# An odd-frequency transform of the sequence's own length in a long convolution, with the order of its pieces rewritten

## The chip, the cores and the metric

The kernel runs on one core of one Trainium2 chip. Its engines are TensorE (PE in the profile; PEld is its weight load), VectorE (DVE), ScalarE (ACT), GpSimd (POOL) and SyncE (SP). The metric is the device time of one execution in microseconds (us), lower is better. All times here are in us unless marked ns, and a place in the profile is the time since the span's first instruction.

## The reference

```python
def _attn_ref(x, h):                      # x (8, 5696, 128), h (5696, 128)
    L = 2 * S
    Xf = np.fft.rfft(x, n=L, axis=1)
    Hf = np.fft.rfft(h, n=L, axis=0)
    y = np.fft.irfft(Xf * Hf[None], n=L, axis=1)[:, :S, :]
    return y

def _moe_ref(x, w_theta, w_tok_r, w_tok_i, w_ch):
    theta = x @ w_theta
    zr, zi = x * np.cos(theta), x * np.sin(theta)
    y = einsum('ts,bsd->btd', w_tok_r, zr) + einsum('ts,bsd->btd', w_tok_i, zi)
    u = x + y
    return u + np.maximum(u @ w_ch, 0.0)
```

A causal convolution along the 5696 positions of each of 8 x 128 sequences comes first, and its result goes through the second block. The change is in the convolution alone.

## The kernel before

**The convolution** is a transform written as matmuls. A sequence is laid out as NB = 89 rows of N2 = 64, zero-padded to NF = 11392 = 178 x 64, and K1 = 90 of the 178 outer frequencies are kept (the sequence is real). A group is two batches and half of the channels (HD = 64), so there are 8 groups, `groups[0]` to `groups[7]`. Each group goes through four stages, each cut into pieces. Every piece takes one PSUM buffer from `psum()`, a pool `fp` of four buffers of two banks each, fills it with matmuls, and has it emptied by one engine:

- **A**, the input pieces (`stage_a`, matmul L251): 16 pieces of 4 matmuls, over the 89 rows. ACT empties them (L258); `on_dve` names pieces that DVE empties instead (L256). Before the change these are pieces 5 and 11 of group 1 and none of a later group.
- **B**, the spectrum pieces (`stage_b` and `f2`, L269): 12 pieces over K1, eight outer frequencies each (the last has two). ACT copies a piece to `xs` (L399), and DVE multiplies it twice with the spectrum of h into `u_t` and `v_t` (L401). Behind the last piece's matmuls, still into that piece's buffer, stand WARM = 12 matmuls whose result is not used (L275).
- **C**, first half of the inverse (`stage_c`, L421 and L422): 16 pieces of 16 matmuls, which read `u_t` and `v_t` over all outer frequencies, so the first C piece waits for the last B piece's DVE products. A piece leaves PSUM multiplied with a table of signs and halves, `sgn`: on DVE as one product (L429), or on ACT as two scaled copies (L426, L427). ACT has pieces 8, 10, 12 and 14, in the last group all eight even ones.
- **D**, second half of the inverse (`stage_d`, L444): 7 pieces, each of which reads all C pieces of its group; ACT empties them into `yt` (L447), and behind the seventh SP stores `yt`.

**The order** is what the loop over groups near L755 writes, and PE, ACT and DVE execute these pieces in that order. `woven` merges lists by giving each entry a place in a share of the stretch. For group g one stretch holds the 16 C pieces of g and the 16 A pieces of g + 1 in the first 55% of it (with `load_x(g + 2)` behind the A pieces), and the next stretch holds the 12 B pieces of g + 1 and the 7 D pieces of g. The first stretch is called C/A here, the second B/D. Before the change the rounds of C/A hold one or two A pieces and a C piece, and B/D runs B0 D0 B1 B2 D1 B3 B4 D2 B5 B6 D3 B7 D4 B8 B9 D5 B10 B11 D6. Three A pieces stand ahead of the first C piece.

`load_x` (L138) brings the next input in 16 transfers on POOL's queue, into a single buffer, so it starts when the A pieces have read the one before.

**After the convolution** the last group's C and D pieces are woven with phase steps (`phase_step`: sines and cosines on ACT, L537 to L539), and the mixing follows: from about 540 us on, PE's matmuls of L1262 and their helpers fill the time.

Of the kernel before, what the change touches and what calls it, by code (L numbers as in the profile page):

```python
# [10 lines left out]
F32 = mybir.dt.float32  # L11
# [12 lines left out]
def kernel(  # L24
# [52 lines left out]

    NF = 2 * S
    N2 = 64
    N1 = NF // N2  # L80
    NB = S // N2
    K1 = N1 // 2 + 1
    KH = K1 // 2
    CK = 8
    HD = D // 2
    EN = N2 // 2 + 1
    WARM = 12
    XP = HD + 4
    assert N1 * N2 == NF and NB * N2 == S and NB % 2 == 1 and K1 <= P
    CHK = [(c0, min(CK, K1 - c0)) for c0 in range(0, K1, CK)]  # L90
    NCK = len(CHK)
    CN = 10
    CHN = [(c0, min(CN, N2 - c0)) for c0 in range(0, N2, CN)]
    UVW = 2 * HD * K1
    hf_hbm = nc.dram_tensor("hf_hbm", (P, HD * K1), F16, kind="Internal").ap()
# [24 lines left out]
    v_t = fc.tile([P, UVW + P], F16)  # L120
    uv = [t[:, :UVW].rearrange("p (e d k) -> p e d k", e=2, k=K1) for t in (u_t, v_t)]
    h16 = s1.tile([P, 2, N2, HD], F16)
# [24 lines left out]
    for p0 in (0, 64):  # L147
# [3 lines left out]
                   allow_small_or_imprecise_dtypes=True)  # L151
    nc.vector.memset(lane[0:64, 2:3], 0.0)
    nc.vector.memset(lane[64:P, 2:3], float(KH))

# [18 lines left out]

    w_t2 = keep.tile([P, K1, 3 * N2], F16, tag="keep", name="w_t2")
    assert WB + BT + 3 * P * 2 <= K1 * 3 * N2
    f1_t = fc.tile([P, 2 * K1], F16)
# [27 lines left out]
    def w_rest(b):  # L204
        s0 = WS * b
        here = w_t2[:, s0:s0 + WS]
        two = here[:, :, :2 * N2].rearrange("p k (f a n) -> p k f a n", f=2, a=2)
        nc.vector.tensor_scalar(two[:, :, :, 1], two[:, :, :, 0], odd, None, op0=mult)
        nc.vector.tensor_scalar(here[:, :, 2 * N2:], here[:, :, :N2], -1.0, None, op0=mult)
        for p0 in (0, 64):  # L210
            nc.vector.tensor_copy(w_t2[p0:p0 + 64, KH + s0:KH + s0 + WS],
                                  w_t2[64 - p0:P - p0, s0:s0 + WS])

    nc.scalar.activation(f1_t[:, :1], zero_b, AF.Sin, bias=zero_b)
    for b in range(len(w_of)):
        index(w_of[b][1], [[1, WS], [N1, 32]], WS * b)
        if b == 0:
            index(f_k, [[1, K1]], 0)
    nc.vector.tensor_scalar(lane[:, 3:4], lane[:, 0:1], 1.0 / NF, None, op0=mult)
    nc.vector.tensor_scalar(o_t, lane[:, 1:2], 0.5, None, op0=mult)  # L220
# [4 lines left out]
    w_turns(0)  # L225
    nc.vector.tensor_scalar(f_t, f_k, lane[:NB, 1:2], 1.0 / N1, op0=mult, op1=mult)
    up(f_t, f_k)
# [32 lines left out]

    def f2(a_st, c, warm=True):

        c0, ck = CHK[c]
        ps = psum()
        for j in range(ck):
            for ri in range(2):
                for e in range(2):
                    rows = slice(64 * e, 64 * e + 64)
                    nc.tensor.matmul(ps[:, e, j * HD:(j + 1) * HD],  # L269
                                     w_t2[rows, slot(e, c0 + j), N2 * (1 - ri):N2 * (3 - ri)],  # L270
                                     a_st["a"][rows, ri * K1 + c0 + j, :],
                                     start=(ri == 0), stop=(ri == 1))
        if c == NCK - 1 and warm:
            for n in range(WARM):
                nc.tensor.matmul(ps[:, n % 2, ck * HD:ck * HD + 384], w_t2[:, 2, :P],  # L275
                                 w_t2[:, 0:2, :].rearrange("p k n -> p (k n)"), start=True, stop=True)
        return ps[:, :, :ck * HD].rearrange("p e (k d) -> p e d k", k=ck)
# [21 lines left out]

    nc.gpsimd.memset(u_t[:, UVW:], 0.0)  # L300
    nc.gpsimd.memset(v_t[:, UVW:], 0.0)
    HS = [(0, 4)] + [(c, 1) for c in range(4, NCK)]
# [21 lines left out]
    def h_chunk(c):  # L324
        c0, ck = CHK[c]
        ps = f2(a_h, c, False)
        nc.scalar.activation(h_part(c)[:, 0], ps[:, 0], AF.Copy, scale=16.0 / NF)
        nc.vector.tensor_scalar(h_later[:, HD * c0:HD * (c0 + ck)].rearrange("p (d k) -> p d k", k=ck),
                                ps[:, 1], 16.0 / NF, None, op0=mult)

# [11 lines left out]
    e_t = fc.tile([P, EN, 2, NB], F16)  # L342
    sgn = fc.tile([P, N2], F32)

    def r_table(n_, r_):
# [9 lines left out]
        sine(k, t, 1)  # L355
        nc.scalar.activation(r_[:, :N2 + EN], k[:, :N2 + EN], AF.Copy, scale=0.125)
        nc.scalar.activation(r_[:, N2 + EN:], k[:, N2 + EN:], AF.Copy, scale=-0.125)

# [10 lines left out]
    def e_index(n, n0, cn):  # L369
        t, k = e_pair(n, cn)  # L370
        index(k, [[1, cn], [N2, NB]], n0)
        nc.gpsimd.tensor_scalar(t, k, lane[:K1, 1:2], 1.0 / NF, op0=mult, op1=mult)
        up(t, k, nc.gpsimd)
# [8 lines left out]

    def s_table():
        half, end = lane[:, 5:6], lane[:, 6:7]
        nc.vector.tensor_scalar(half, lane[:, 1:2], 0.0, -0.5, op0=ALU.is_equal, op1=mult)
        nc.vector.tensor_scalar(end, lane[:, 1:2], float(K1 - 1), -0.5, op0=ALU.is_equal, op1=mult)
        nc.vector.scalar_tensor_tensor(half, half, 1.0, end, op0=add, op1=add)
        nc.vector.memset(sgn, 1.0)
        nc.vector.tensor_scalar(sgn[:, :EN], sgn[:, :EN], half, None, op0=mult)
        nc.vector.tensor_scalar(sgn[:, EN:], sgn[:, EN:], odd, half, op0=mult, op1=mult)  # L390

    def stage_b(a_st, warm, refill):

        def chunk(c):
            c0, ck = CHK[c]
            hv = h_part(c)
            ps = f2(a_st, c, warm)
            xs = fs.tile([P, 2, HD, CK], F16, tag="xs", name="xs")
# [11 lines left out]

    def stage_c(st, last):
        sg = sgn[:K1].unsqueeze(2).unsqueeze(1).to_broadcast([K1, 2, N2, 8])

        def chunk(q):
            if q == 0:
                st["g"] = fg.tile([P, 2 * N2, P], F16, tag="g", name="g_")
            ps = psum()
            for i in range(8):
                o = ps[:, i // 4, (i % 4) * P:(i % 4 + 1) * P]
                at = (q + i) * K1  # L420
                nc.tensor.matmul(o, u_t[:, at:at + P], r_u, start=True, stop=False)  # L421
                nc.tensor.matmul(o, v_t[:, at:at + P], r_v, start=False, stop=True)  # L422
            g_out = st["g"][:K1, :, q:q + 8].rearrange("p (r n) q -> p r n q", r=2)
            g_in = ps[:K1].rearrange("p a (q r n) -> p r n (a q)", q=4, r=2)
            if q % 16 == 0 and (last or q >= 64):
                nc.scalar.mul(g_out[:, :, :EN], g_in[:, :, :EN], sgn[:K1, 0:1])  # L426
                nc.scalar.mul(g_out[:, :, EN:], g_in[:, :, EN:], sgn[:K1, EN:EN + 1])  # L427
            else:
                nc.vector.tensor_tensor(g_out, g_in, sg, op=mult)  # L429
        return [lambda q=q: chunk(q) for q in range(0, 2 * HD, 8)]  # L430

    def stage_d(st, bp, dh, then=None):
        def chunk(n0, cn):
# [5 lines left out]
            for j in range(cn):  # L439
                n = n0 + j  # L440
                o = ps[:, j // nq, (j % nq) * NB:(j % nq + 1) * NB]
                for ri in range(2):
                    e_ = e_t[:K1, n, ri, :] if n < EN else e_t[:K1, N2 - n, ri, ::-1]
                    nc.tensor.matmul(o, g_[:K1, ri * N2 + n, :], e_, start=(ri == 0), stop=(ri == 1))  # L444
# [15 lines left out]
    def front(g, on_dve=()):  # L460
# [4 lines left out]
        steps, a_st = stage_a(lambda q: x16[:NB, :, q], on_dve)  # L465
        return steps, stage_b(a_st, g > 0, dh == 0 and groups[g + 1][1] == 1)

# [13 lines left out]
    for n, f in enumerate(a0):  # L481
        f()
        if n == 9:
# [4 lines left out]
    in_order.enter_context(tc.manual_schedule(engines={mybir.EngineType.DVE, mybir.EngineType.Activation}))  # L488
    woven(b0, ([s_table, lambda: r_table(0, r_u), lambda: r_table(1, r_v)], 0.0, 0.6),
          [])  # L490
    e_left = [lambda f=f, n=n: f(*E_STEPS[n]) for f, n in (
# [117 lines left out]
    def open_ring():  # L609

        ring["all"] = keep.tile([P, K1 * 3 * N2], BF16, tag="keep", name="ring")
        pump()
# [142 lines left out]
    for g, (bp, dh) in enumerate(groups):  # L755
        st = {}
        last = g + 1 == len(groups)
        if last:
            late_order.enter_context(tc.manual_schedule(engines={mybir.EngineType.Pool}))
        a_, b_ = front(g + 1, () if g else (5, 11))  # L760
        if last:
            for _ in range(3):
                steps0.pop(0)()
        now = [with_load(steps0.pop(0), n < 6) for n in range(9)] if last else []
        c_ = stage_c(st, last)
        if g + 2 < len(groups):
            a_ = a_ + [lambda g=g: load_x(g + 2)]
        woven((c_, 0.06 if a_ else 0.0, 1.0), (a_, 0.0, 0.55), now, ([] if g else e_left, 0.0, 0.9))
        if g == 0:
# [6 lines left out]
        now = [steps0.pop(0) for _ in range(3)] if last else []  # L776
        woven(b_, (stage_d(st, bp, dh, load_ya1 if last else None), 0.0, 1.1 if b_ else 1.0), now)
        if g + 2 == len(groups):
# [546 lines left out]
```

## Time and profile before

| | us |
|---|---|
| three timed runs | 2033.98, 2034.99, 2040.38 |
| their median | 2034.99 |
| the profiled execution, its own time | 2035.64 |
| span of that execution, first to last instruction | 2033.9 |
| convolution up to the first C piece (set-up, spectrum of h, group 0's A and B) | 0 to 66.5 |
| group 0: C/A, then B/D | 66.5 to 89.7, then to 109.9 |
| groups 1 to 5, first C piece to first C piece | 37.4, 39.1, 38.4, 37.2, 37.2 |
| group 6: C/A, then B/D and three phase steps | 299.2 to 317.9, then to 338.3 |
| group 7: C pieces with phase steps | 338.3 to 367.5 |
| the granted TensorE clock, mean of the span | 0.987 |

The first table row of the profile says that PE is busy for 1936.4 of 2033.9 us and DVE for 1573.3. Most of that is the mixing; a group of the convolution is a stretch where PE is full and a stretch where it isn't, which the rows by stretch in the prediction show. In such a row each engine has its busy time and its number of instructions, and PEclk is the share of the full TensorE clock that was granted.

### The profile page before, as it was taken

How to read it: one execution, taken by the hardware profiler on the slowest of the kernel's cores; microseconds unless marked ns; L12 is line 12 of the kernel's file. 1: busy time of each engine (PE TensorE's matmuls, PEld its weight loads, DVE VectorE, ACT ScalarE, POOL GpSimd, SP SyncE). 2: the span in 40 equal slices, each digit the busy share in tenths (PEclk: the TensorE clock that was granted, in tenths of full speed). 3: DMA queues.
4: the chain of work that ended last, by engine and by line, in shares of the span. 5: the costliest groups of instructions: out<-in, count | busy, mean ns of one | idle time of the engine just before them, and what ended most of it. 6: DMA issues, size and time to landing. Idle time of an engine off the chain costs nothing.

```text
span 2033.9 us, 41286 instructions
## 1 busy us (share of the span) xinstructions
PE 1936.4 (95%) x15664; PEld 1073.2 (53%) x15841; DVE 1573.3 (77%) x2890; ACT 655.1 (32%) x1004; POOL 964.0 (47%) x1721
## 2 busy tenths in 40 slices
PE   6799999788999999999999999999999999999998
PEld 5688888654444444444444444444444444444444
DVE  8777778786788888888877669768677786777767
ACT  6788888851232323333210000011111111111111
POOL 8523322363364545455565554553545445354450
PEclk9799999998999999999999999999999999999999
DMA  9978975997898998989999899887878878788793
GB/s 115 64 84 124 89 87 165 266 272 139 163 174 177 174 178 154 180 170 181 171 168 164 121 241 243 131 149 129 152 135 146 149 129 144 137 146 147 133 157 85
DMA packets 487752, 312.05 MB, mean 153 GB/s; under 512 B 182887, under 2 KB 448615, under 8 KB 486567
## 3 DMA queue, kind: packets, MB, share of 16 engines
q0 software_dynamic: 321600, 155.29, 60.8%
q1 hardware_dynamic: 158784, 140.34, 24.0%
q10 hardware_dynamic: 7168, 13.76, 1.9%
q8 instruction: 124, 2.03, 0.4%
q14 instruction: 76, 0.62, 0.1%
HBM read 354.37 MB, written 90.29 MB: 219 GB/s over the span
## 4 chain that ended last, share of the span: by engine, by line
PE 66%; DMA 3%; DVE 3%; issue 1%; POOL 0%; ACT 0%; DVEq 0%; ACTq 0%
PE m L1262 62%; DMA b<-z_hbm 2%; DVE c L1269 1%; PE v L942 1%; PE utp L935 1%; PE m L1266 1%; PE m L1150 1%; DVE wt L855 1%; PE theta_ps L515 0%; PE tpz L883 0%; DMA yT<-yt_hbm 0%; PE m L1183 0%; POOL ring L631 0%; DMA ring<-in_moe_w_tok_r_dram 0%; DMA ring<-in_moe_w_tok_i_dram 0%
## 5 line engine op out<-in xcount | busy, mean ns | idle before, releaser
L631 POOL DMA_DIRECT2D ring<-in_moe_w_tok_i_dram x720 | 390.2, 552 | 652.8 <-DVE wt L855 554.0
L855 DVE STREAM_TRANSPOSE wt<-ring 128x384 f32<-128x384 f32 (+2 forms) x720 | 358.9, 523 | 115.1 <-PE m L1262 63.7
L631 POOL DMA_DIRECT2D ring<-in_moe_w_tok_r_dram x720 | 388.5, 553 | 124.8 <-DVE wt L855 79.5
L1262 PE MATMUL m<-b,wt 128*128 128x512 bf16 x1605 | 384.8, 379 | 4.1 <-DVE wt L855 2.1
L1262 PEld LDWEIGHTS <-wt 128*128 128x128 bf16 x1804 | 176.0, 98 | 216.4 <-DVE wt L855 5.1
L1269 DVE TENSOR_TENSOR c<-c,m 128x512 f32<-128x512 f32 x412 | 265.3, 669 | 0.4 <-PE m L1262 0.4
L937 ACT ACTIVATE ring<-utp 128x512 bf16<-128x512 bf16 x85 | 50.8, 597 | 575.8 <-PE utp L935 575.8
L138 POOL DMA_DIRECT2D x<-in_x_dram x128 | 99.6, 807 | 140.4 <-PE ps L251 132.8
L421 PE MATMUL ps<-r_u,u_t 128*128 128x128 f16 x1024 | 124.6, 220 | 6.9 <-DVE u_t L401 3.5
L1183 PE MATMUL m<-b,wt 128*128 128x512 bf16 x471 | 113.1, 387 | 12.0 <-DMA b<-zr_hbm 8.1
L422 PE MATMUL ps<-r_v,v_t 128*128 128x128 f16 x1024 | 123.6, 220 | 0.3
L932 ACT ACTIVATE ub<-c 128x512 bf16<-128x512 f32 x88 | 55.1, 628 | 185.8 <-DMA ring<-in_moe_w_tok_i_dram 103.8
L422 PEld LDWEIGHTS <-v_t 128*128 128x128 f16 x1024 | 100.6, 98 | 5.6 <-issue 4.2
L421 PEld LDWEIGHTS <-u_t 128*128 128x128 f16 x1024 | 100.6, 98 | 4.7 <-DVE u_t L401 4.7
L399 ACT ACTIVATE xs<-ps 128x1024 f16<-128x1024 f32 x96 | 91.5, 982 | 8.8 <-PE ps L269 2.6
L1183 PEld LDWEIGHTS <-wt 128*128 128x128 bf16 x528 | 51.5, 99 | 71.0 <-issue 17.1
L401 DVE TENSOR_TENSOR u_t<-xs,hs 128x1024 f16<-128x1024 f16 x96 | 64.2, 669 | 31.7 <-ACT xs L399 29.3
L885 ACT ACTIVATE ring<-tpz 128x512 bf16<-128x512 bf16 (+1 forms) x46 | 27.5, 597 | 148.8 <-PE tpz L883 123.7
L517 ACT ACTIVATE red<-theta_ps,magic 128x512 f32<-128x512 f32 (+1 forms) x46 | 31.6, 687 | 127.1 <-PE theta_ps L515 99.4
L269 PEld LDWEIGHTS <-w_t 64*128 64x128 f16 x3240 | 60.4, 102 | 22.0 <-issue 15.8
L401 DVE TENSOR_TENSOR v_t<-xs,hs 128x1024 f16<-128x1024 f16 x96 | 63.7, 664 | 0.0
L944 DVE SCALAR_TENSOR_TENSOR c<-v,c 128x512 f32<-128x512 f32 x88 | 59.9, 682 | 2.9 <-PE v L942 2.6
(2932 smaller groups left out, 3773.3 us busy)
## 6 DMA issues: line engine op xcount, KB each, us to landing
ring<-in_moe_w_tok_r_dram POOLq DMA_DIRECT2D x352, 96.0 KB, 4.6
ring<-in_moe_w_tok_i_dram POOLq DMA_DIRECT2D x352, 96.0 KB, 4.9
ring<-in_moe_w_tok_r_dram POOLq DMA_DIRECT2D x352, 80.0 KB, 4.4
ring<-in_moe_w_tok_i_dram POOLq DMA_DIRECT2D x352, 80.0 KB, 3.8
cp_hbm<-c SPq DMA_DIRECT2D x88, 256.0 KB, 2.3
c<-cp_hbm SPq DMA_DIRECT2D x88, 256.0 KB, 4.5
out_dram<-c SPq DMA_DIRECT2D x88, 256.0 KB, 4.2
yy<-y_hbm SPq DMA_DIRECT2D x84, 128.0 KB, 2.5
```

Of the source, the lines that this page charges most:

```text
L138: nc.gpsimd.dma_start(x16[p0:p1, e, n0:n0 + 16, :HD], bass.AP(tensor=src.tensor, offset=src.offset + (p0 * N2 + n0) * D + dh * HD, ap=[[N2 ...
L269: nc.tensor.matmul(ps[:, e, j * HD:(j + 1) * HD], w_t2[rows, slot(e, c0 + j), N2 * (1 - ri):N2 * (3 - ri)], a_st["a"][rows, ri * K1 + c0 + ...
L399: nc.scalar.activation(xs[:, :, :, :ck], ps, AF.Copy)
L401: nc.vector.tensor_tensor(uv[r][:, :, :, c0:c0 + ck], xs[:, :, :, :ck], hv[:, r:r + 1].to_broadcast([P, 2, HD, ck]), op=mult)
L421: nc.tensor.matmul(o, u_t[:, at:at + P], r_u, start=True, stop=False)
L422: nc.tensor.matmul(o, v_t[:, at:at + P], r_v, start=False, stop=True)
L631: nc.gpsimd.dma_start(wb[32 * i:32 * i + 32, :ng, :nj * 64], bass.AP(tensor=a.tensor, offset=a.offset + row0 * S + p * H + i * QR + j0 * 6 ...
L855: nc.vector.transpose(wt.rearrange("p j t r -> p (j t r)").bitcast(F32).rearrange("p (j g t) -> p g j t", j=TJ, g=4)[:, :ng, :nj], wb[:, : ...
L944: nc.vector.scalar_tensor_tensor(c[:m], v[:m], 0.0, c[:m], op0=ALU.max, op1=ALU.add)
L1183: nc.tensor.matmul(ms[n // 2 * 2 + h], a[n][:, j, :, r], bts_of[p][jj][n % 2 * 2 + h][:, r, :], start=(n % 2 == 0 and jj == 0 and r == 0), ...
L1262: nc.tensor.matmul(ms[q], a[q][:, j, :, r], bts[jj][q][:, r, :], start=(jj == 0 and r == 0), stop=(jj == NJ - 1 and r == 1 and q not in left))
L1269: nc.vector.tensor_tensor(c, z, ms[q], op=op)
```

## The change

The transform is taken at the odd quarter frequencies of a transform of length 5696 = 89 x 64, whose outer frequencies k1 + 1/4 are all 89 kept; no signs and halves remain, so a C piece leaves PSUM as a plain copy. K1 becomes 89, while `u_t` and `v_t` keep a pitch of KP = 90 with a column that POOL zeroes. The last B piece has one outer frequency in place of two. The tables of angles get a quarter added, and `s_table` with `sgn` goes. In the order, for groups from 1 on, the A pieces lie in the first 34% of C/A with pieces 3, 6, 9, 12 and 15 on DVE; ACT has the even C pieces from 4 on (six of them); a D piece follows every second B piece, with the rest behind the last; and the unused matmuls, now 8, stand ahead of the first C piece of groups 1 to 6.

```diff
-    NF = 2 * S
-    N1 = NF // N2
-    K1 = N1 // 2 + 1
-    KH = K1 // 2
+    K1 = NB
+    KP = K1 + 1
+    KH = KP // 2
+    QUARTER = 0.25
-    WARM = 12
+    WARM = 8
...
-    def f2(a_st, c, warm=True):
+    def f2(a_st, c):
...
-        if c == NCK - 1 and warm:
-            for n in range(WARM):
-                nc.tensor.matmul(ps[:, n % 2, ck * HD:ck * HD + 384], w_t2[:, 2, :P],
-                                 w_t2[:, 0:2, :].rearrange("p k n -> p (k n)"), start=True, stop=True)
...
+    for t in uv:
+        nc.gpsimd.memset(t[:, :, :, K1:], 0.0)
...
-    def s_table():
-        half, end = lane[:, 5:6], lane[:, 6:7]
...
-    def stage_c(st, last):
-        sg = sgn[:K1].unsqueeze(2).unsqueeze(1).to_broadcast([K1, 2, N2, 8])
+    def stage_c(st, g, last):
         def chunk(q):
...
             ps = psum()
+            if q == 0 and g and not last:
+                for n in range(WARM):
+                    nc.tensor.matmul(ps[:, n % 2, :384], w_t2[:, 2, :P],
+                                     w_t2[:, 0:2, :].rearrange("p k n -> p (k n)"), start=True, stop=True)
...
-            if q % 16 == 0 and (last or q >= 64):
-                nc.scalar.mul(g_out[:, :, :EN], g_in[:, :, :EN], sgn[:K1, 0:1])
-                nc.scalar.mul(g_out[:, :, EN:], g_in[:, :, EN:], sgn[:K1, EN:EN + 1])
+            if q % 16 == 0 and (last or q >= (32 if g else 64)):
+                nc.scalar.activation(g_out, g_in, AF.Copy)
             else:
-                nc.vector.tensor_tensor(g_out, g_in, sg, op=mult)
+                nc.vector.tensor_copy(g_out, g_in)
...
-    woven(b0, ([s_table, lambda: r_table(0, r_u), lambda: r_table(1, r_v)], 0.0, 0.6),
-          [])
+    woven(b0, ([lambda: r_table(0, r_u), lambda: r_table(1, r_v)], 0.0, 0.6))
...
-        a_, b_ = front(g + 1, () if g else (5, 11))
+        a_, b_ = front(g + 1, (3, 6, 9, 12, 15) if g else (5, 11))
...
-        woven((c_, 0.06 if a_ else 0.0, 1.0), (a_, 0.0, 0.55), now, ([] if g else e_left, 0.0, 0.9))
+        woven((c_, (0.02 if g else 0.06) if a_ else 0.0, 1.0), (a_, 0.0, 0.34 if g else 0.55), now,
+              ([] if g else e_left, 0.0, 0.9))
...
-        woven(b_, (stage_d(st, bp, dh, load_ya1 if last else None), 0.0, 1.1 if b_ else 1.0), now)
+        d_ = stage_d(st, bp, dh, load_ya1 if last else None)
+        if last:
+            woven(d_, now)
+        else:
+            for n, f in enumerate(b_):
+                f()
+                if n % 2 and n < NCK - 1:
+                    d_.pop(0)()
+            for f in d_:
+                f()
```

## The prediction

> **What bounds the kernel now.** First the chain of waits, to see what the convolution's time is worth:
>
> ```profile
> PE 66%; DMA 3%; DVE 3%; issue 1%; POOL 0%; ACT 0%; DVEq 0%; ACTq 0%
> ```
>
> It is PE's, nearly all of it the mixing (L1262, 62%), and no mixing matmul runs before the convolution's last group is done, so a microsecond gained or lost in the convolution shifts everything behind it. Then the busy time by stretch, for the C/A and B/D stretches of groups 1 and 2 and three windows I cut out of B/D (columns: stretch and length, busy time and instructions of PE, PEld, DVE, ACT, POOL, then the clock):
>
> ```profile
> 109.90:128.70 18.80, 18.71 (x308) 18.48 (x308) 13.68 (x12) 15.14 (x23) 6.78 (x9) 1.00 0.81 108
> 128.70:147.20 18.50, 15.78 (x514) 13.56 (x512) 15.38 (x25) 17.42 (x22) 5.23 (x8) 1.00 0.83 54
> 147.20:166.00 18.80, 18.66 (x308) 18.47 (x308) 13.73 (x13) 15.02 (x23) 6.30 (x9) 1.00 0.77 106
> 166.00:186.30 20.30, 16.77 (x515) 14.75 (x513) 15.66 (x25) 17.08 (x21) 5.73 (x8) 0.92 1.17 143
> ...
> 94.17:97.58 3.41, 1.67 (x76) 1.39 (x72) 2.88 (x6) 3.38 (x5) 0.18 (x1) 1.00 1.43 91
> ...
> 97.58:101.00 3.42, 3.38 (x84) 3.16 (x85) 2.20 (x4) 2.42 (x3) 0.00 (x0) 0.50 0.03 6
> ```
>
> C/A is PE's: 18.7 of 18.8, with ACT (15.1) and DVE (13.7) both slack. B/D is ACT's: 17.4 of 18.5, and PE could do it in much less. The last two rows are a clock dip: a window in which PE was busy only 1.67 of 3.41, then one at half clock. Third, ACT in time order at both ends of group 1's B/D, where its idle time is, and PE at the start:
>
> ```profile
> 129.44 1.02 ACT L399 ACTIVATE xs<-ps 128x1024 f16<-128x1024 f32 x1 [0.26 <-ACT g__2352 L427]
> 131.27 0.92 ACT L447 ACTIVATE yt<-ps 128x890 bf16<-128x890 f32 x1 [0.81 <-PE ps L444]
> ```
> ```profile
> 143.77 0.91 ACT L447 ACTIVATE yt<-ps 128x890 bf16<-128x890 f32 x1
> 144.56 1.38 ACT L399 ACTIVATE xs<-ps 128x1024 f16<-128x1024 f32 x2
> 145.80 0.45 ACT L447 ACTIVATE yt<-ps 128x356 bf16<-128x356 f32 x1
> ```
> ```profile
> 130.18 1.00 PE L444 MATMUL ps<-e_t,g__2352 90*128 90x89 f16 x20 [0.83 <-DVE g__2352 L429]
> ```
>
> D0 waits for DVE's last C piece (128.81 to 130.03), and ACT, with B0 emptied, waits 0.81 for D0. Last, what it costs to empty a piece:
>
> ```profile
> L429 DVE TENSOR_TENSOR g__2352<-ps,sgn 90x1024 f16<-90x1024 f32 x12 | 14.6, 1221 | 5.2 <-PE ps L422 5.2
> L426 ACT ACTIVATE g__2352<-ps,sgn 90x528 f16<-90x528 f32 x4 | 2.8, 697 | 1.7 <-PE ps L422 1.6
> L427 ACT ACTIVATE g__2352<-ps,sgn 90x496 f16<-90x496 f32 x4 | 2.6, 658 | 0.0
> L256 DVE CAST a__1317<-ps 128x720 f16<-128x720 f32 x2 | 1.8, 896 | 0.0
> L733 DVE COPY ring<-ps 128x512 bf16<-128x512 bf16 x22 | 9.2, 418 | 2.9 <-PE ps L532 2.8
> ```
>
> **The copy that replaces the product** (L429) is in no row. The nearest is L256: same operation, same types, from PSUM: 896 ns for 720 elements. The product's 1221 for 1024 lies on one line with it, (1221 - 896)/304 = 1.07 ns an element and 0.13 fixed, so I take **1.22: DVE gains nothing**. The other end is L733's 418 ns for 512, from a 16-bit source: half the rate per element, 0.69 for 1024 by doubling the part above 0.13. On ACT two copies (started 0.60 and 0.66 apart, 1.26) become one of 1024 elements, like L399, whose starts are 0.92 apart: 0.33 saved each, where ACT is what lacks.
>
> **(a) A pieces in the first third, +2.2 in each of groups 1 to 6.** The merged order is A0 A1 A2 C0 A3 A4 A5 C1 ... A12 A13 A14 C4 A15 C5: four pieces a round, and there are four PSUM buffers. PE's own time is 0.89 for a C piece (starts at 111.70 and 112.60) and 0.32 for an A piece (two in 0.63). Before, a round of two A pieces and a C piece left a buffer to spare. Now, when three A pieces have gone by (0.96), the next C piece needs C0's buffer or one freed no sooner, and that comes after 0.17 (the last matmul's end after the next could start) + 0.04 + 1.22 + 0.07 (semaphores, as between rows) = 1.50. PE idles 0.54 ahead of C1, C2, C3 and C4: 2.2. DVE itself isn't the bound: C and one A piece take 1.22 + 0.82 of a 2.40 round. From C5 on the stretch is as before. Six groups: **+13.0**.
>
> **(b) D pieces behind every second B piece, -1.7 in each B/D of groups 0 to 6.** B1 takes the place in which ACT waited, -0.81. D5 (0.83 between starts) is emptied behind the last B piece, so off the path to the first C piece, -0.83; the last B piece is half as wide, -0.1. What was first in C/A now waits a little for ACT: the A pieces' buffers, covered by the wait of C0 for DVE's `v_t`. SP's store of `yt` still follows D6 and whatever refill of the spectrum is ahead of it. Seven times: **-11.9**.
>
> **(c) The unused matmuls.** In B/D, 12 of them (143.13 to 145.25) were free: PE waited 0.74 behind them at 147.28. Taken away: 0, at most -0.3 where ACT's last `xs` waited for them (1.4 in all under L275). Ahead of C0, 8 at 0.163 are 1.30. PE reaches C0's buffer only when ACT has emptied D6, and 0.37 of the 1.30 lies in the remaining wait for `v_t`. So +0.93, six times: **+5.6**.
>
> **(d) Clock dips.** Three B/D stretches hold a half-clock window (97.6, 179.5, 213.6). Each follows a window with PE busy 1.67, 1.82 or 1.76 of 3.41; windows with 2.35 and more aren't followed by one. Groups 2 and 3 are 39.1 and 38.4 where an undisturbed one is 37.2, so a dip costs 1.1 to 1.8. The low windows hold stalls of PE called "issue" (1.6 to 1.8) while the x transfers run. These start behind A15, at C0 + 10.8 (5 x 0.89 + 13 x 0.32 + 2.2) where it was + 11.2, on a POOL queue that is idle then; with C/A longer by 2.2 they end 2.6 earlier against B0. I take one dip fewer: **-1.5** (bounds: all three gone, -4.2; all seven stretches, see the second rival).
>
> The Trainium skill (TensorE: Matmul & The Clock Gate, "Why this matters for your kernels") has the clock fall after a whole idle window, and asks only for no idle gap above about 3 us. By that rule no B/D stretch would dip, before or after, and (d) would be 0. Here the clock fell after gaps of 1.6 to 1.8 in half-busy windows, so the measurement decides.
>
> **(e) Set-up, -0.8.** `s_table` is 1.1 of DVE (48.1 to 49.05) in a stretch where `xs` waits for DVE; two 0.15 operations on `lane` come ahead of the first table. POOL's two memsets of a column cost nothing: POOL idles 0.9 before the x transfers at 44.2 and nobody waits for it; uncovered they would be some 0.5 (2 x 0.24 of L300 and L301).
>
> **(f) ACT's cheaper C pieces.** Groups 1 to 6: 0, ACT has 3.7 of slack in C/A. Group 0: 4 x 0.33, where PE waits for L426 and L427 and DVE (0.82, 1.17), I take -0.9. Group 7: 8 x 0.33 = 2.6 in a stretch where ACT is busy 28.4 of 29.3; but DMA is full there (share 1.06) and PE then waits 4.85 for a store at 397.4, so between 0 and -2.6; I take the middle, **-1.3**. Together -2.2.
>
> 178 for 180 columns and 89 for 90 frequencies: under 0.1 a group, left out.
>
> **Sum**: 13.0 - 11.9 + 5.6 - 1.5 - 0.8 - 2.2 = +2.2. The span of 2033.9 becomes 2036.1; the execution itself took 2035.64, and the median of the runs is 2034.99, to which I add: **2037.2**. A steady group becomes 37.2 + 2.2 - 1.7 + 0.9 = 38.6.
>
> **Rivals.** *No wait for a buffer.* If DVE copies at the rate of L733, the chain in (a) is 0.17 + 0.04 + 0.69 + 0.07 = 0.97 against 0.96, and the 13.0 vanish: 2024.2. L256 speaks against it, as do 12 products at 1221 in each group; for it, that no row shows this very copy. 22%.
>
> *The half clock in every B/D stretch* (slower). Place: the 3.41 windows of B/D. A round of two B pieces and a D piece keeps ACT 2.66 and PE 1.7, so PE is at 64% without a stall; the densest part, the 12 unused matmuls, leaves. All seven stretches have an "issue" stall (0.8 to 1.8). It decides from PE busy below about 2.0 of 3.41, that is a stall of 0.9 that PE can't make up inside one window. Four more dips and the one not saved, 5 x 1.5 = +7.5: 2044.7. For it: three of seven already; against it: four weren't, with stalls of 0.8 to 1.1. 20%.
>
> *The new order of D gains half.* If PE's stalls rather than ACT end B/D, only D0's wait goes: -0.8 in place of -1.7, +6.3: 2043.5. Against it, ACT is busy without a gap from 131.3 to the end in group 1; for it, ACT's gaps of 0.6 to 1.1 in groups 2 and 3. 12%.
>
> **How the numbers follow.** The forecast has 46%, with its own range 2031 to 2043 (d and f at their bounds). What a measurement of this kernel can tell from no change is about 0.3%, 6.1 us: 2028.9 to 2041.1. Faster: most of the first rival and a little of the forecast, 0.22. Slower: 0.16 of the second, 0.08 of the third and 0.06 of the forecast, 0.30. Same: 0.48. The range reaches to the rivals' times: 2024 to 2046.
>
> **What will show it.** (a): L421 idle about 0.5 ahead of four C pieces a group, ended by DVE's copy, and the copy's mean at 1.22; C/A at 21 rather than 18.8. (b): no idle ACT at the first `yt`, B/D at about 17.7. (c): L275 right ahead of L421, in a C/A that doesn't start earlier for it. (d): windows of clock 0.50 counted. Wrong if C/A stays under 19.5, if a group comes below 37, or if the difference lies behind 380 us.

## The result, and the profile after

The changed kernel takes 2047.14 us (median of six runs, 2044.42 to 2049.62) beside 2036.18 for the kernel before (six runs, 2033.98 to 2040.38). The ratio is **1.0053, 95% interval 1.0042 to 1.0064**: slower by 11.0 us where the forecast had 2.2, and above the range.

The chain of waits says what it said before: PE and its mixing lead.

```profile
PE 67%; DMA 3%; DVE 2%; issue 1%; POOL 0%; ACT 0%; ACTq 0%; DVEq 0%
```

So the loss must lie in the convolution. From the first C piece of group 0 to that of group 7 it takes 286.8 us instead of 271.8 in the profiled executions; everything behind that takes 1.7 less, the set-up 0.7 less. The busy time by stretch (columns as before: stretch and length, then PE, PEld, DVE, ACT, POOL, clock), for C/A and B/D of groups 1 and 2, then three windows at the end of group 0's B/D:

```profile
110.10:131.50 21.40, 20.12 (x309) 19.47 (x307) 15.10 (x14) 11.42 (x14) 9.32 (x13) 0.94 0.89 94
131.50:149.90 18.40, 15.20 (x508) 13.44 (x506) 16.27 (x25) 17.89 (x23) 2.62 (x4) 1.00 0.58 43
149.90:170.40 20.50, 18.97 (x308) 18.34 (x307) 15.11 (x14) 12.06 (x16) 8.81 (x12) 1.00 0.92 106
170.40:190.30 19.90, 16.38 (x510) 14.58 (x508) 16.28 (x25) 18.18 (x23) 3.12 (x5) 0.91 0.94 136
102.25:105.67 3.42, 2.21 (x66) 2.08 (x64) 3.02 (x6) 3.41 (x5) 0.00 (x0) 1.00 0.00 0
105.67:109.08 3.41, 3.33 (x17) 2.27 (x17) 2.45 (x4) 3.41 (x6) 0.00 (x0) 0.50 0.27 58
109.08:112.50 3.42, 3.42 (x26) 2.77 (x24) 0.36 (x1) 0.26 (x1) 0.00 (x0) 0.50 0.99 213
```

C/A went from 18.8 to 20.5 where the clock stays at 1.00 and to 21.4 where it doesn't. (These rows begin and end up to 0.2 ahead of the matmuls that bound a stretch.) B/D, cut at the same matmuls in both kernels, fell only from 18.57 to 18.38 in group 1, which no half clock disturbed. The half clock now lasts two windows and reaches into C/A. What PE does there, in time order:

```profile
105.57 2.26 PE L253 MATMUL ps<-f_t,x 89*128 89x178 f16 x12 [0.38 <-ACT xs L390]
107.62 2.77 PE L410 MATMUL ps<-w_t 128*128 128x384 f16 x8
110.18 0.31 PE L415 MATMUL ps<-r_u,u_t 128*128 128x128 f16 x1
```

The eight unused matmuls (L410) take 2.77 at half clock and stand right ahead of C0, whose last input, DVE's `v_t`, was ready at 108.12. Next, what a piece costs to empty, from the groups by line and shape:

```profile
L422 DVE CAST g__3293<-ps 89x1024 f16<-89x1024 f32 x10 | 12.2, 1221 | 5.6 <-PE ps L416 5.6
L420 ACT ACTIVATE g__3293<-ps 89x1024 f16<-89x1024 f32 x6 | 6.1, 1019 | 4.5 <-PE ps L416 4.5
L392 DVE TENSOR_TENSOR v_t<-xs,hs 128x128 f16<-128x128 f16 x8 | 8.1, 1017 | 0.0
L392 DVE TENSOR_TENSOR u_t<-xs,hs 128x128 f16<-128x128 f16 x7 | 5.3, 754 | 0.0
L390 ACT ACTIVATE xs<-ps 128x128 f16<-128x128 f32 x7 | 5.3, 761 | 0.0
```

The copy on DVE is 1221 ns, as taken. The last three rows are the last B piece: half the elements of before, at 1.8 to 2.6 times the price. Before, the three were

```profile
L401 DVE TENSOR_TENSOR u_t<-xs,hs 128x256 f16<-128x256 f16 x8 | 3.1, 389 | 0.3 <-ACT xs L399 0.3
L401 DVE TENSOR_TENSOR v_t<-xs,hs 128x256 f16<-128x256 f16 x8 | 3.1, 385 | 0.0
L399 ACT ACTIVATE xs<-ps 128x256 f16<-128x256 f32 x7 | 3.0, 426 | 1.5 <-PE ps L275 1.4
```

Last, PE's waits from the first C piece of group 0 to that of group 7 (total, times, longest):

```profile
PE ps L271 <- issue: 4.7, 6, 1.5
PE ps L437 <- issue: 4.0, 5, 2.5
...
PE ps L415 <- DVE g__3293 L422: 1.5, 4, 0.4
```

The C pieces wait three or four times 0.38 a group for a buffer; "issue" is time in which PE waited for nothing the profile shows, up to 2.5 at once, where the kernel before had at most 1.8.

### The profile page after: what moved, and what is told of

It reads as the page before. It is cut to its first block, busy times and chain, and to the rows that moved or that the text cites. A ratio compares the mean times of both kernels' runs of the same rounds, so it can differ in the third digit from the quotient of the medians.

```text
span 2046.4 us, 41281 instructions
## 1 busy us (share of the span) xinstructions
PE 1946.5 (95%) x15769; PEld 1074.0 (52%) x15769; DVE 1584.8 (77%) x2904; ACT 637.3 (31%) x950; POOL 962.4 (47%) x1723
## 4 chain that ended last, share of the span: by engine, by line
PE 67%; DMA 3%; DVE 2%; issue 1%; POOL 0%; ACT 0%; ACTq 0%; DVEq 0%
PE m L1264 62%; DMA b<-z_hbm 2%; DVE c L1271 1%; PE v L944 1%; PE utp L937 1%; PE m L1268 1%; DVE wt L857 1%; PE theta_ps L507 0%; PE tpz L885 0%; PE m L1152 0%; PE m L1185 0%; DMA ring<-in_moe_w_tok_i_dram 0%; POOL ring L623 0%; DMA y_hbm<-ring 0%; DMA ring<-in_moe_w_tok_r_dram 0%
## 5 line engine op out<-in xcount | busy, mean ns | idle before, releaser
L1185 PEld LDWEIGHTS <-wt 128*128 128x128 bf16 x528 | 50.6, 98 | 69.0 <-issue 13.7
L392 DVE TENSOR_TENSOR u_t<-xs,hs 128x1024 f16<-128x1024 f16 x96 | 67.1, 699 | 18.9 <-ACT xs L390 16.2
L392 DVE TENSOR_TENSOR v_t<-xs,hs 128x1024 f16<-128x1024 f16 x96 | 68.8, 717 | 0.0
L253 PE MATMUL ps<-f_t,x 89*128 89x178 f16 x512 | 55.2, 255 | 8.9 <-ACT xs L390 3.0
```

The source lines that it names most:

```text
L253: nc.tensor.matmul(ps[:, i // 2, (i % 2) * 2 * K1:(i % 2 + 1) * 2 * K1], lhs(q + i), f1_t[:NB], start=True, stop=True)
L392: nc.vector.tensor_tensor(uv[r][:, :, :, c0:c0 + ck], xs[:, :, :, :ck], hv[:, r:r + 1].to_broadcast([P, 2, HD, ck]), op=mult)
L1185: nc.tensor.matmul(ms[n // 2 * 2 + h], a[n][:, j, :, r], bts_of[p][jj][n % 2 * 2 + h][:, r, :], start=(n % 2 == 0 and jj == 0 and r == 0), ...
```

## The experiments

One table for all runs. Ratio: to the kernel before, timed beside each, with its 95% interval. The other columns are from one profile each: seven groups (C0 of group 0 to C0 of group 7), the median C/A and the shortest B/D of groups 1 to 6, PE's idle time under "issue", and the time at half clock, both from the end of group 0's C/A to C0 of group 7. C/A is counted here from the start of its first C matmul to the start of its last, B/D from there to the next C0. One profile is one execution, and executions of one kernel lie up to 14 us apart. A difference in us is that of two ratios times 2036, and is uncertain by about 0.0015, 3 us.

| kernel | ratio | seven groups | C/A | B/D | issue | half clock |
|---|---|---|---|---|---|---|
| before | 1 | 271.8 | 18.6 | 18.6 | 11.5 | 10.2 |
| after | 1.0053 (1.0042 to 1.0064) | 286.8 | 21.3 | 18.2 | 9.9 | 23.9 |
| e1_warm_back | 1.0011 (1.0001 to 1.0022) | 279.8 | 20.9 | 17.5 | 9.1 | 17.1 |
| e2_even_piece | 1.0026 (1.0016 to 1.0036) | 278.8 | 20.4 | 18.2 | 10.9 | 13.7 |
| e3_a_spread | 1.0026 (1.0014 to 1.0038) | 278.1 | 18.9 | 18.7 | 13.9 | 20.5 |
| e4_d_old | 1.0078 (1.0063 to 1.0094) | 287.4 | 20.6 | 19.4 | 7.9 | 10.2 |
| e5_no_warm | 1.0041 (1.0021 to 1.0061) | 284.6 | 22.4 | 17.4 | 8.8 | 41.0 |
| e6_before_d | 0.9986 (0.9973 to 0.9999) | 272.1 | 18.8 | 17.3 | 15.3 | 17.1 |
| e7_even_spread_back | 1.0003 (0.9990 to 1.0016) | 279.6 | 19.3 | 18.6 | 18.2 | 17.1 |
| e8_even_back | 1.0012 (0.9999 to 1.0025) | 274.0 | 20.4 | 17.3 | 12.0 | 3.4 |
| e9_before_nox | 0.9992 (0.9983 to 1.0001) | 268.7 | 18.6 | 18.6 | 2.2 | 3.4 |
| e10_before_d_nox | 0.9966 (0.9952 to 0.9979) | 264.1 | 18.5 | 17.3 | 6.9 | 3.4 |
| e11_after_nox | 1.0020 (1.0011 to 1.0030) | 278.8 | 20.3 | 18.2 | 1.1 | 13.7 |
| e12_rest_nox | 0.9973 (0.9962 to 0.9985) | 266.1 | 19.0 | 17.3 | 4.7 | 6.8 |
| e13_paced | 1.0030 (1.0018 to 1.0042) | 277.1 | 19.3 | 17.3 | 18.3 | 13.7 |
| e14_balanced | 0.9988 (0.9978 to 0.9998) | 273.7 | 18.6 | 18.2 | 16.3 | 17.1 |
| e15_early_balanced | 0.9978 (0.9969 to 0.9988) | 270.3 | 18.2 | 18.7 | 8.3 | 6.8 |
| e16_paced_balanced | 1.0022 (1.0012 to 1.0032) | 273.5 | 18.6 | 17.7 | 17.1 | 13.7 |
| e17_early_narrow | 0.9982 (0.9973 to 0.9991) | 271.9 | 18.2 | 19.0 | 7.6 | 6.8 |
| e18_early_d_old | 0.9996 (0.9985 to 1.0007) | 274.0 | 18.2 | 19.7 | 5.4 | 3.4 |

### Undoing one part of the change

**The unused matmuls** back behind the last B piece:

```diff
-    WARM = 8
+    WARM = 12
...
+        if c == NCK - 1 and warm:
+            for n in range(WARM):
+                nc.tensor.matmul(ps[:, n % 2, ck * HD:ck * HD + 384], ...)
...
-            if q == 0 and g and not last:
-                for n in range(WARM): ...
```

> The changed kernel with the unused matmuls as they were before the change: 12 behind the last B piece, none ahead of C0. Theory 'clock' (the half-clock windows that now reach from the end of B/D into C/A, 6.8 us long where they were 3.4, are the main miss; they come because no dense matmuls stand at the end of B/D any more): the windows shrink to 3.4 us again, which gives back half of (6.83+3.41+6.83+6.83) - 3 x 3.41 = 13.7, so 6.8 us, and the 8 unused matmuls ahead of C0 no longer add 0.93 x 6 = 5.6: 2047.1 - 6.8 - 5.6 = 2034.7. Theory 'place' (only the 5.6 of the place is to be had, the dips come anyway): 2041.5. Theory 'narrow piece' (the width-1 last B piece holds C0 back, and the unused matmuls hide under it wherever they stand): 2046 to 2048.

Measured 1.0011, 8.6 us less than the change: more than the place alone (5.6), less than place and clock (12.4). Half clock 23.9 to 17.1, and it lies elsewhere: in the change three of the four half-clock stretches start 4.3 to 4.7 us ahead of C0, in e1 none less than 9.5 ahead. It is the largest single part.

**The width of the last B piece**:

```diff
-    CHK = [(c0, min(CK, K1 - c0)) for c0 in range(0, K1, CK)]
+    CHK = [(c0, min(CK, KP - c0)) for c0 in range(0, KP, CK)]
...
+            k = min(c0 + j, K1 - 1)
...
```

> The changed kernel with a last B piece of width 2: the spectrum's padding column is computed as a copy of the last one, so its buffer is written in pairs (256 elements in place of 128 per partition); no output depends on that column. Theory 'narrow piece': xs goes from 760 to about 424 ns, u and v from 753 and 1017 to about 389 each, yt beside it from 1.26 to 0.92, and C0 starts about 1.0 earlier in 7 groups: 2047.1 - 7 = 2040. Theory 'clock' alone: the copies change but the path at the end of B/D is PE's at half clock, 2045 to 2047. The prediction's own term (a narrower piece is 0.1 cheaper per group) would have it at 2047.8.

Measured 1.0026, 5.5 us less. The same three instructions, now in pairs:

```profile
L389 ACT ACTIVATE xs<-ps 128x256 f16<-128x256 f32 x8 | 3.4, 421 | 0.2 <-DVE v_t L391 0.2
L391 DVE TENSOR_TENSOR u_t<-xs,hs 128x256 f16<-128x256 f16 x8 | 3.2, 396 | 0.0
L391 DVE TENSOR_TENSOR v_t<-xs,hs 128x256 f16<-128x256 f16 x8 | 3.1, 391 | 0.0
```

Twice the elements in 421, 396 and 391 ns in place of 761, 754 and 1017. But the shortest B/D is unchanged (18.2): in an undisturbed group, it seems, the unused matmuls ahead of C0 hid the narrow copies. What the width gained lies in the half-clock time, 23.9 to 13.7, and in C/A, which no window runs into any more.

**A's placement**:

```diff
-        a_, b_ = front(g + 1, (3, 6, 9, 12, 15) if g else (5, 11))
+        a_, b_ = front(g + 1, () if g else (5, 11))
...
-        woven((c_, (0.02 if g else 0.06) if a_ else 0.0, 1.0), (a_, 0.0, 0.34 if g else 0.55), now, ...
+        woven((c_, 0.06 if a_ else 0.0, 1.0), (a_, 0.0, 0.55), now, ...
```

> The changed kernel with A's pieces in groups 1 to 6 placed as before the change (over the first 55% of C, all emptied by ACT). Theory 'buffer wait' (A's pieces in the first third make PE wait for buffers, the prediction's +2.2 per group; a simulation-free count from the trace is 4 waits of 0.38 = 1.5 per group): C/A falls from about 21.3 to about 19.5, 6 x 1.6 = 9.6, 2037.5. Theory 'only moved' (ACT then is the engine that is late, and the waits appear in another place): 2045 to 2049.

Measured 1.0026, 5.5 us less. The buffer waits went (C/A 18.9), yet not 9.6 but 5.5 came of it: the idle time under "issue" rose from 9.9 to 13.9.

**D's order**, the old weave in the changed kernel:

```diff
-            for n, f in enumerate(b_):
-                f()
-                if n % 2 and n < NCK - 1:
-                    d_.pop(0)()
...
+        woven(b_, (d_, 0.0, 1.1 if b_ else 1.0), now)
```

> The changed kernel with the old weave of B and D (D's pieces spread over 1.1 of B's length). The prediction's term for the new order is -1.7 per group: if it holds, undoing it gives 2047.1 + 11.9 = 2059. Rival 'half' (D's new order gains half): 2053. Theory 'order brings the dips' (the D pieces now stand one right behind the other at the end of B/D, with no B piece to fill PE between their buffer waits, and the clock drops there): the gain is eaten by the dips, 2045 to 2049, and the 6.8 us windows at the end of B/D are gone.

Measured 1.0078, 5.1 us more: a gain of less than half of the 11.9. The half-clock time is that of the kernel before, 10.2.

**No unused matmul at all** (both places empty):

```diff
-    WARM = 8
...
-            if q == 0 and g and not last:
-                for n in range(WARM): ...
```

> The changed kernel without any unused matmul (the 8 ahead of C0 go, none behind the last B piece). Numbers as a ratio to the kernel before, where the changed one stands at 1.0053. Theory 'on the path' (the unused matmuls only stand between A2 and C0, 0.93 in each of 6 groups, and warm nothing that matters): -5.6 us, ratio 1.0026. Theory 'clock' (they are what ends a half-clock window, since they are the one dense stretch there): without them the half-clock windows in groups 1 to 7 grow from 23.9 us in all to 30 or more and eat what is saved, ratio 1.005 or above. The place behind the last B piece gave 1.0011; if that run gained because the matmuls left C0, this one must reach it too.

Measured 1.0041 (1.0021 to 1.0061): the time can't tell it from the change, nor one theory from the other. The half clock speaks for "clock": 41.0 us, and C/A at 22.4. Of the three places the half clock is longest with none of them, and shortest with them behind the last B piece.

### One part alone, and several

D's order alone, in the kernel before:

```diff
-        woven(b_, (stage_d(st, bp, dh, load_ya1 if last else None), 0.0, 1.1 if b_ else 1.0), now)
...
+            for n, f in enumerate(b_):
+                f()
+                if n % 2 and n < NCK - 1:
+                    d_.pop(0)()
...
```

> The kernel before with one part of the change alone: a D piece behind every second B piece, in place of D spread over 1.1 of B's length. Everything else (real transform of double length, A over 55% of C, 12 unused matmuls behind the last B piece, a last B piece of width 2) as before. The prediction's term, -1.7 per group in 7 groups, gives 2036.2 - 11.9 = 2024.3, ratio 0.994. From the clean groups of the changed kernel with the even piece (18.24 with 0.93 of unused matmuls in front of C0, against 18.62) it is -1.3, so 2027, ratio 0.9955. Rival 'block loads' (PE waits at boundaries of 256 of its instructions for the load of the next block, and a shorter B/D only waits longer there): half, ratio 0.998 or above, with the idle time under 'issue' up from 11.5 us in the first eight groups.

Measured 0.9986: 2.9 us of 11.9. B/D reached 17.3, 1.3 less, where nothing disturbed it; elsewhere PE stopped, for longer than anywhere before (PE in time order, group 2, with the unused matmuls of a dip behind it):

```profile
179.21 1.56 PE L269 MATMUL ps<-a__3317,w_t 64*128 64x64 f16 x51 [3.45 <-issue]
...
183.50 2.63 PE L275 MATMUL ps<-w_t 128*128 128x384 f16 x12
```

The even piece with the unused matmuls back (the edits of e1 and e2), and that with A spread as well (of e1, e2 and e3):

> The changed kernel with the even last B piece (width 2) and the 12 unused matmuls back behind it, none ahead of C0. Theory 'two prices' (the narrow piece and the place of the unused matmuls each cost by themselves): -5.4 and -8.5 add, ratio 1.0053 - 0.0027 - 0.0042 = 0.9984. Theory 'one price' (both act through the same stretch ahead of C0: the narrow copies hold C0 back and the unused matmuls hide under them): no better than the better of the two, 1.001. With it half-clock windows in groups 1 to 7 of 3.4 us each and C/A of 20.4 or less are expected.

> The changed kernel with the even last B piece, the 12 unused matmuls back behind it, and A's pieces of groups 1 to 6 over the first 55% of C on ACT alone: of the change are left the complex transform of own length and the new order of D. If the placement of A's pieces costs 1.6 per group on top (C/A 18.86 in place of 20.45), it is 9.6 us below the kernel with only the first two: ratio 0.9937 where that one is at 0.9984. If what C/A gives is taken back in B/D, as it was in the run with A's pieces alone put back (C/A -1.6, B/D +1 to +2, ratio 1.0026 in place of 1.0005), it is within 3 us of it.

Measured 1.0012 and 1.0003. The first is "one price": width and place act through the same stretch, and together they give what the place gives. The second took C/A from 20.4 to 19.3 and paid for it with 18.2 us under "issue", more than any kernel before it.

### What "issue" is

Counting PE's instructions (matmuls, weight loads and the few that only wait, in order of start) up to the end of each such stall over 0.3 us, in the kernel before:

```
ended at  97.6   137.2   173.8   178.6   211.9   251.5   255.5   287.1   323.1   326.5
count     2755   4546    6084    6339    7618    9412    9668    10946   12483   12740
step / 256        7.00    6.01    1.00    5.00    7.01    1.00    4.99    6.00    1.00
```

Every step lies within two of a multiple of 256 (a few records of a trace can be missing). And there is one DMA queue of this row of the page (queue, packets, MB, share):

```profile
q8 instruction: 124, 2.03, 0.4%
```

124 packets of 16 KB, 64 bytes for each of 256 instructions. Each of the 12 stalls under "issue" ends 1.3 to 1.7 after such a packet has landed. Beside idle queues such a packet starts about 1.1 us after PE has passed a boundary, takes 0.9 to 1.7, and PE goes on over the next boundary no sooner than 1.2 after it has landed: in these two kernels no 256 instructions of the convolution go by in less than 3.4. Beside the input load (q0) it starts up to 2.4 after the boundary in the kernel before, up to 3.2 in the changed one. C/A takes 7 us for 256 instructions; B/D, with its small matmuls, 3.4 to 5. So B/D is where it stops, and the input load runs into B/D in both kernels.

The Trainium skill (Runtime: NRT & Kernel Launch, "Instruction fetch mechanics") has the same blocks of 16 KiB and 256 instructions and calls the cost of a boundary mostly hidden. The trace agrees with the size, not with the hiding: 11.5 us in seven groups.

The test is to leave the later input loads out: groups 2 to 7 transform group 1's input again.

```diff
-            a_ = a_ + [lambda g=g: load_x(g + 2)]
+            x16s[g + 2] = x16s[g + 1]
```

> The kernel before with the input loads of groups 2 to 7 left out (these groups transform group 1's input again), so that queue q0 is idle in every B/D stretch after group 0. Theory 'block loads' (PE stops at a boundary of 256 of its instructions until the next block of 16 KB has come through queue q8; that load starts 1.0 us after a boundary when no input load runs and 1.3 to 3.8 after it beside one): the idle time under 'issue' in groups 0 to 6 falls from 11.5 to about 6 us and the time by about 4 us, ratio 0.998. Theory 'issue is not from the transfers': idle and time unchanged, ratio 1.000.

> The kernel before with the new order of D and with the input loads of groups 2 to 7 left out. With them the new order gave 0.9986 in place of the 0.994 of the prediction, with 15.3 us under 'issue'. Theory 'block loads': without them that idle falls to about 7 us and the order gets what its clean groups show, 1.3 in each of 7 groups: 9 us below the one without the order, ratio about 0.9935. Theory 'clock' (the half-clock windows take it back, whatever the transfers do): 3 us below, ratio 0.9965.

> The changed kernel with the input loads of groups 2 to 7 left out. Theory 'block loads': 9.9 us under 'issue' fall to about 5, ratio 1.0053 - 0.0025 = 1.003; as in the kernel before, so the block loads take as much from both and are no part of the distance between them. If the changed kernel gains clearly more than the kernel before does without its loads, the earlier input load of the changed kernel (it starts 11.6 us after C0 and now overlaps the first third of B/D) is a part of the loss.

> The changed kernel with the even last B piece, the 12 unused matmuls back behind it, A's pieces spread over 55% of C, and the input loads of groups 2 to 7 left out. With the loads it was at 1.0003 with 18.2 us under 'issue', the most of all. Theory 'block loads': 9 us or more come off, ratio 0.996 or below. Theory 'clock': 4 us as in the kernel before, 0.998.

Measured 0.9992, 0.9966, 1.0020 and 0.9973. The idle time fell from 11.5 to 2.2, 15.3 to 6.9, 9.9 to 1.1 and 18.2 to 4.7; here the kernel before (first line) and with the load left out (second):

```profile
PE ps L269 <- issue: 7.3, 9, 1.8
```
```profile
PE ps L269 <- issue: 2.1, 4, 0.9
```

Half-clock windows went with it, most of them (10.2 to 3.4, 17.1 to 3.4, 23.9 to 13.7, 17.1 to 6.8). In time that is 1.6 us for the kernel before, 4.1 with D's order, 6.7 for the change and 6.1 for e12. "Block loads" holds: what delays PE is the input load. Its worth was overstated for the kernel before, whose shortest B/D is 18.6 with and without the load: of 9.3 us less idle, 1.6 came off the time, and that is not clear of noise. Without loads D's order is worth 5.3, between "clock" and "block loads"; with them it was 2.9, and the two are no further apart than the noise. What the order did to the wait of C0, without loads, the old order first, then the new:

```profile
PE ps L421 <- DVE u_t L401: 4.5, 7, 0.9
```
```profile
PE ps L421 <- DVE u_t L401: 0.9, 1, 0.9
```

In six of seven groups C0 no longer waits for DVE. In group 2 it is PE itself that sets C0 now: from the first unused matmul on it does 12 of those, D5, D6 and three A pieces without a pause, from 179.51 to C0 at 183.80. Between the change and the kernel before, 1.0053 became 1.0020 against 0.9992: about half of the distance goes with the loads.

### The load's pace and its place

Pacing, two memsets on POOL behind each transfer:

```diff
+                    if g > 1:
+                        for _ in range(2):
+                            nc.gpsimd.memset(pace, 0.0)
```

> The kernel with the even last piece, the unused matmuls back behind it and A spread (1.0003 with its input loads, 0.9973 without), with the same 16 input loads of a group, but two small memsets on POOL behind each, so that one load starts about every 1.4 us in place of 0.75 and q0 is half as busy for twice as long. Theory 'queue' (the next 256 PE instructions come late because the 16 DMA engines are full of the input load's small packets): the load of a block starts 1.0 to 1.5 us after its boundary everywhere, the idle time under 'issue' falls from 18.2 to about 9 us, ratio about 0.9985. Theory 'bytes' (what delays the blocks is the traffic as such): the delay is smaller and lasts longer, 18 us under 'issue' stay, ratio 1.000.

Measured 1.0030, and inconclusive for its question. POOL in time order:

```profile
149.71 13.81 POOL L146 MEMSET pace<- 128x288 f32 x35
166.58 8.97 POOL L140 DMA_DIRECT2D x<-in_x_dram  x12 [3.06 <-PE ps L258]
```

The memsets ran ahead of the transfers, which followed each other as closely as ever, only later: PE waited 9.5 us for input. Whether a thinner load would do less harm stays open.

Emptying A and C by both engines in turn, alone and with the memsets:

```diff
-            if q % 16 == 0 and (last or q >= (32 if g else 64)):
+            if q % 16 == 0 and (last or g or q >= 64):
...
-        a_, b_ = front(g + 1, () if g else (5, 11))
+        a_, b_ = front(g + 1, (2, 4, 6, 8, 10, 12, 14) if g else (5, 11))
```

> The same kernel, unpaced, with every second piece of A (7 of 16) and every second piece of C emptied by the other engine in groups 1 to 6: DVE 7 A and 8 C, ACT 9 A and 8 C. Theory 'buffer wait' (PE's waits in C/A are for the engine that has most to empty): C/A falls from 19.3 to about 18.6, by 0.7 in 6 groups: 4 us, ratio 0.998. Theory 'block loads' (what C/A gives is taken back in B/D): 1.000, with more than 18 us under 'issue'.

> Both steps of the first two kernels of this call together: paced input loads, and A and C emptied in turn. If 'queue' and 'buffer wait' both hold, their gains add: 0.9985 - 0.002 = 0.9965, below both kernels. If only one holds, the better of the two.

Measured 0.9988 and 1.0022. C/A fell to 18.6 as expected, 3 us came of it, about as much as the uncertainty; the second repeats the memsets' loss.

An earlier load, with A in the first quarter on top of e8, and A and C in turns by the edit of e14:

```diff
-        woven((c_, (0.02 if g else 0.06) if a_ else 0.0, 1.0), (a_, 0.0, 0.34 if g else 0.55), now, ...
+        woven((c_, 0.06 if a_ else 0.0, 1.0), (a_, 0.0, 0.25 if g else 0.55), now, ...
```

> The changed kernel with the even last piece and the unused matmuls back behind it, A's pieces in the first quarter of C and emptied by ACT and DVE in turn, C's pieces in turn as well. The input load of the next group then starts about 9 us after C0 in place of 11 to 12 and is over by 22 to 23, so only some 2 to 4 us of it lie beside B/D. Theory 'block loads': idle time under 'issue' below 8 us (12.0 with A in the first third), half-clock windows in two groups at most, ratio 0.998. Theory 'buffer wait' (A this early makes PE wait for buffers by more than is saved): C/A 20 or more and ratio 1.001 or above.

Measured **0.9978 (0.9969 to 0.9988): faster than both kernels**, 4.5 us below the one before and 15 below the change. Group 2's two stretches:

```profile
145.37:163.60 18.23, 17.67 (x299) 17.48 (x296) 13.42 (x13) 12.39 (x15) 10.67 (x15) 1.00 1.20 127
163.60:182.29 18.69, 16.79 (x528) 14.68 (x526) 16.77 (x27) 17.94 (x23) 1.29 (x2) 1.00 0.75 113
```

C/A is the shortest so far, with A in the first quarter: early A pieces cost nothing when both engines empty A and C in turn. POOL's column shows the load: 10.67 of its issue in C/A, 1.29 left for B/D. "Issue" is at 8.3, and 3.3 of that is one stop in group 3.

On this quiet ground two of the terms that had failed were undone once more, with the edits of e2 and e4 turned round:

> The kernel with A early and in turns (0.9978), but with the narrow last B piece of the change (width 1). Theory 'narrow piece' (its copies of 760, 753 and 1017 ns stand between the last B piece and C0): +0.6 to +1.0 in 7 groups, 4 to 7 us, ratio 0.9998 to 1.0012. Theory 'one price' (behind 12 unused matmuls the narrow copies are hidden): 0.998.

> The kernel with A early and in turns (0.9978), but with the old weave of B and D. Theory 'block loads' (the order of D is worth 1.3 to 1.4 in each of 7 groups once PE's block loads are on time): +9 us, ratio 1.0025. The prediction's term of 1.7 would give +12, ratio 1.0037. Theory 'half' (the order is worth half in any surroundings; made alone in the kernel before it brought 2.9 us, undone in the changed kernel it cost 5.1): ratio 1.000.

Measured 0.9982 and 0.9996. The narrow piece costs 0.3 in a group's B/D and nothing that the time shows, once the unused matmuls stand behind the last B piece: "one price". D's order is worth 1.0 in a group and 3.7 us in all: "half".

## Why the prediction was wrong

**(b) D's order, -11.9: the step that failed.** Of the -1.7 a group, the shortest B/D shows 1.0 to 1.3. Over seven groups that would be 7 to 9; the runs show 2.9 (before against e6), 5.1 (e4 against the change), 5.3 (e9, e10) and 3.7 (e18, e15). Two things were missed, the second of them in part only argued. The prediction took D5 off the path to C0 because ACT empties it later, but PE still computes D5 between the last B piece and C0; once C0 no longer waits for DVE (seven waits in e9, one in e10), PE's own work is the next limit. And it treated PE's stalls called "issue" as given. They are block loads that PE waits for; when ACT's waits are taken away, PE comes to the next boundary sooner and stops there: 15.3 us in e6 in place of 11.5 (1.9 of it in six stops of 0.32 at a D piece that fall on no boundary), and 17.1 at half clock in place of 10.2. In time, what the loads alone take from the order isn't shown: 2.9 with them and 5.3 without lie within the noise. Even without them two of the seven groups, 3 and 6, gained nothing, with a stop of 1.8 and one of 2.2. The rival "gains half" came nearest in size and had the condition right that PE's stalls end B/D, but not the split: an undisturbed group gains 1.0 to 1.3 and not 0.8.

**(c) and (d), +5.6 and -1.5.** Together 4.1 was taken and 8.6 measured (e1). Taking the unused matmuls out of B/D was costed at nothing because PE waited behind them. But they were what kept the window at the end of B/D dense. In the changed kernel:

```profile
143.22:146.63 3.41, 2.42 (x71) 2.21 (x69) 3.16 (x6) 3.41 (x5) 0.00 (x0) 1.00 0.02 5
225.13:228.55 3.42, 2.40 (x64) 2.17 (x57) 3.02 (x6) 3.42 (x6) 0.00 (x0) 1.00 0.02 5
266.10:269.51 3.41, 2.31 (x68) 2.11 (x66) 3.08 (x5) 3.41 (x4) 0.00 (x0) 1.00 0.02 5
```

In three groups PE is busy 2.2 to 2.4 there (the last two rows, and the window at 102.25 above), in pieces that wait 0.2 to 0.7 each, mostly for ACT, and half clock follows, with the eight moved matmuls inside it at 2.77 in place of 1.3. That clock would dip once less was wrong: four stretches dip, three of them twice as long. The rival "half clock" put its point at PE busy 2.0 of 3.41; dips came after 2.21, 2.31 and 2.40 as well. They did not after 2.42, nor after 2.35 in the kernel before, so busy time alone doesn't decide.

**The last B piece, -0.1 a group** inside (b), had the wrong sign: a piece of single elements costs more than one of pairs. It decided no undisturbed group but went with the half clock: 5.5 us undone alone (e2), nothing the time shows with the unused matmuls behind it (e17).

**(a) A early, +13.0.** The mechanism was right: four waits of 0.38 (0.54 predicted) and C/A at 20.45 where the clock held, +1.8 a group. Undone alone it gave 5.5, with more "issue" time in B/D (9.9 to 13.9). That (a) came out low hid part of the miss in (b), (c) and (d), which for the sum was luck. It was no price of early pieces as such: shared out in turn, even earlier ones cost nothing (e15).

**(e)** fits: the first C piece starts 0.72 earlier in these two profiles, and 0.9 earlier by the medians of four profiles with the old set-up (66.2 to 68.7) and fourteen with the new one (64.7 to 69.2; the two with memsets left out), though they scatter by more than that. **(f)** can't be seen by itself; group 7's C pieces took 0.5 less where -1.3 was taken, and group 0's C/A came out no shorter.

"No wait for a buffer" fell at once: the copy took 1221 ns. Three figures of the prediction don't come out of its own rows, and none of them decides anything: the 0.69 is 0.13 + 2 x 0.29 = 0.71, 48.1 to 49.05 is 0.95 and not 1.1, and (d) and (f) at their bounds give 2033 to 2041, not 2031 to 2043. Undone one by one, the four parts (the place, the width, A, D's order) give 8.6 + 5.5 + 5.5 - 5.1 = 14.5, more than the 11.0 there are; they act on each other (the first two undone together gave 8.3 and not 14.1), so no split is exact. Whether the complex transform itself costs or saves can't be told: e7 and e6 differ by it (and by small things) and lie 0.0017 apart with an uncertainty of 0.0018.

## What to carry to other kernels

Where an engine's idle time is called "issue", count its instructions: if the stalls fall on one step, what is late is the code, and what helped here was to move bulk transfers out of the stretch with the small instructions. Matmuls that do no work may be holding the clock; before moving them, look at what is left in the window that they filled. A piece that is taken off one engine's path may still stand on another's. A gain read from one undisturbed group counts in full only if the next limit behind it doesn't stop the same engine.

## What the runs showed of the hardware

- PE takes its code in blocks of 256 instructions, and in the convolution of the two kernels no block went by in under 3.4 us. A packet of code started up to 2.7 us later beside the input load than beside idle queues (3.8 us after the boundary in e7, against 1.1). The prediction had taken these stalls as given.
- The clock halved even after a window in which PE never idled for more than 0.4 us at a time (0.38, 0.29 and 0.23 in 225.1 to 228.6 of the changed kernel, busy 2.40 of 3.41). The Trainium skill (TensorE: Matmul & The Clock Gate, "A second HAM failure mode: psum-queue depth-cycling") tells of a clock that oscillates when PE idles briefly but often between groups; the trace agrees.
- Writing 128 elements of 16 bits one by one at a step took longer than writing 256 in pairs: 761 against 421 ns on ACT, 754 and 1017 against 396 and 391 on DVE.
